# The first pair's q and k cut in halves on two DMA queues, and the order of loads behind them, in a fused attention and cosine feed-forward kernel

## The chip, the cores and the metric

The kernel runs on one core of one Trainium2 chip. The metric is device microseconds of one execution, compared as medians of several runs. A profile is one further execution, recorded instruction by instruction; its own time and its span stand in the table below.

## The reference

Eight batches, 12 heads, 448 positions, head size 64. Queries and keys are normalized, scores are divided by tau = 0.1, and the attention output, laid out as 3584 rows of 768, goes through a feed-forward layer whose activation is h times cos(h).

```python
def _attn_ref(q, k, v, tau):
    q_n = q / (norm(q, axis=-1, keepdims=True) + 1e-06)
    k_n = k / (norm(k, axis=-1, keepdims=True) + 1e-06)
    scores = matmul(q_n, k_n.transpose(0, 1, 3, 2)) / tau
    attn = exp(scores - max(scores))
    attn = attn / (sum(attn, axis=-1, keepdims=True) + 1e-09)
    return matmul(attn, v)                       # (8, 12, 448, 64)

def _moe_ref(x, w_in, w_out):                    # x: (3584, 768)
    h = x @ w_in                                 # (3584, 2048)
    return (h * cos(h)) @ w_out                  # (3584, 768)
```

Inputs and output are float32 in HBM.

## The kernel before

**Work and tiles.** Two heads make a *pair*, three pairs a *unit* (`UP = 3`), two units a batch. There are 16 units and 48 pairs; a label such as `scale1.0` means unit 1, pair 0 of it, which is pair 3 of the kernel. A pair's k lies in partitions 0 to 63 of a buffer `raw` and its q in partitions 64 to 127, seven positions of each head to a partition (`NB = 7`). For each pair the steps are:

- `load`: one DMA for k and one for q (224 KB each), from SyncE's queue (SP);
- `square` (`sq`), `reduce` (`n2`) and `rnorm` (`rn`): the squares, their sums over 64 elements, and one over the root of these. The squares of the first three pairs are taken by ScalarE (ACT), those of the next three by GpSimd (POOL), as the plan's entry `sq` says; the sums by VectorE (DVE); the root by ScalarE as Ln and then Exp, or, for the units that the entry `roots` names, by GpSimd with a power;
- `scale`: raw times rn, to `qks` in bf16, by GpSimd. For pair 0 VectorE does the second half (three of seven position blocks; the first half has four);
- `transposes`: by TensorE (PE) through the identity for the first nine pairs, copied from PSUM to `qkT` by VectorE; by a transposing DMA from pair 9 on;
- `scores`: four score steps per pair, each followed by an Exp of ScalarE into `PX` (one of 448 columns, three of 896);
- `attend`: PX times V, and the row sums. For the first pairs the sums are inverted by ScalarE (`lnS`, `expS`), spread over the partitions by a matmul on PE (`spread`, label B) and multiplied in by VectorE, which gives the transposed attention output `xT`.

After the six pairs of a batch, `m1` multiplies `xT` with the first weights `W1` (16 blocks of 128 of its columns), ScalarE takes the cosine, VectorE multiplies to `gT`, and the second product (`m2_fill`, `m2_quarters`) with the second weights `W2` is spread over the next batch's pairs as filling between their scores. V, W1 and W2 are converted to bf16 on the way in by DMAs from GpSimd's queue: V one DMA per half of the partitions and unit, W1 and W2 in four pieces each.

**What sets the order.** The program records its operations with what they read and write (`Program.op`), and `Program.play` simulates them with costs, among them constants for DMA queues, and picks for each engine the next operation by readiness and due time (`late`, moved by `bias`). `emit` writes each engine's instruction stream in that order, with semaphore waits. So a changed constant or entry can change the order of any engine, and an engine never passes an instruction that waits. Where PE would be idle in the opening stretch, filler matmuls on zeros are put in.

**The opening.** SP issues k and q of pairs 0 to 5, twelve DMAs. ScalarE begins with its table load, then squares pair 0. GpSimd's first DMAs are V of unit 0, held until pair 0's q has landed (tile `first`); behind its half of `scale0.0` it issues V of unit 1 and W1's first piece, then goes on with `scale0.1`.

```python
    first = ["first"]
    load_v(0, None, first)
    first = [("qks", 0, 0, 0)]
    load_w1(0, None, first)
    load_w1(1, None, first)
    load_v(1, None, first)
```

## Time and profile before

| what | value |
|---|---|
| median of 3 runs | 415.97 us (415.55 to 416.21) |
| profiled execution, its own time | 415.4 us |
| its span, first to last instruction | 413.6 us |
| TensorE busy | 404.6 us, 98% |
| ScalarE busy | 270.2 us, 65% |
| GpSimd busy | 248.5 us, 60% |
| VectorE busy | 199.9 us, 48% |
| granted TensorE clock | 1.000 |
| DMA moved | 63.99 MB, mean 155 GB/s |

The profiled execution is 0.57 us under the median; 1.8 us of it lie outside the span. TensorE's busy time includes the fillers of the opening. In a timeline row the first number is the start in us from the span's start, the second the duration, then the engine, the line of the kernel, the operation and its tiles, and in brackets the idle time before it with what ended that. SPq and POOLq are queues in which an engine issues DMAs. In a row of the stretches view each engine has its busy time in the stretch and the number of its instructions. In a row of DMA issues the last number is the median time in us from issue to landing.

### The profile page before, as it was taken

The page shows a single profiled execution, that of the slowest core. Times are in us where ns is not written, and L with a number is a line of the kernel's source. Part 1 is how long each engine was busy: PE and PEld are TensorE (multiplying, and loading weights), DVE is VectorE, ACT ScalarE, POOL GpSimd, SP SyncE. Part 2 cuts the span into 40 slices and gives each one's busy share as a digit, 9 for nine tenths or more (in the row PEclk, how much of TensorE's full clock was granted, in tenths as well). Part 3 has the DMA queues.
Part 4 walks back from the last instruction along what each step waited for, and adds up shares of the span by engine and source line. Part 5 has one row for each costly group of instructions (what it writes and reads, how often), then busy time and mean ns, then how long its engine had stood idle before and what let it go on. Part 6 is the DMA issues. An engine that isn't in the chain of part 4 may idle for free.

```text
span 413.6 us, 13910 instructions
## 1 busy us (share of the span) xinstructions
PE 404.6 (98%) x6213; PEld 243.8 (59%) x6213; DVE 199.9 (48%) x279; ACT 270.2 (65%) x384; POOL 248.5 (60%) x196
## 2 busy tenths in 40 slices
PE   7899999999999999999999999999999999999997
PEld 3354556655566655765567656865567655655555
DVE  4574653426664457445644567344742344413421
ACT  5897578985889745985497647884488745623500
POOL 4999995894776985988489656946482303020000
PEclk9999999999999999999999999999999999999999
DMA  8999999489997999586988975797933531151023
GB/s 183 248 252 226 207 222 202 136 157 215 178 163 164 228 258 188 121 205 149 206 101 188 268 132 113 135 215 188 169 51 79 147 85 32 46 139 38 2 73 81
DMA packets 78736, 63.99 MB, mean 155 GB/s; under 512 B 41844, under 2 KB 72404, under 8 KB 78676
## 3 DMA queue, kind: packets, MB, share of 16 engines
q1 hardware_dynamic: 60468, 50.42, 54.4%
q0 software_dynamic: 18048, 12.59, 20.7%
q8 instruction: 49, 0.80, 0.8%
q10 hardware_dynamic: 160, 0.10, 0.1%
q14 instruction: 11, 0.09, 0.1%
HBM read 55.44 MB, written 11.19 MB: 161 GB/s over the span
## 4 chain that ended last, share of the span: by engine, by line
PE 91%; POOL 3%; ACT 2%; DVE 2%; DMA 1%; issue 0%; SPq 0%; ACTq 0%; POOLq 0%
PE MP L1052 27%; PE SC L953 20%; PE AV L953 12%; PE SC L727 7%; PE AV L764 5%; PE MP L1081 4%; PE AV L788 4%; PE SC L1081 3%; PE MP L953 2%; PE AV L837 2%; POOL qks L678 1%; PE SC L735 1%; ACT cosb L982 1%; PE MP L852 1%; PE AV L1081 1%; DMA raw<-in_q_dram 1%
## 5 line engine op out<-in xcount | busy, mean ns | idle before, releaser
L742 ACT ACTIVATE PX<-SC 128x448 bf16<-128x448 f32 (+1 forms) x192 | 148.7, 825 | 16.0 <-PE SC L727 10.9
L1052 PE MATMUL MP<-W,gT 64*64 64x384 bf16 x2816 | 136.2, 323 | 0.7 <-DVE qkT L716 0.6
L1052 PEld LDWEIGHTS MP<-W,gT 64*64 64x64 bf16 x2816 | 80.1, 107 | 34.5 <-issue 3.9
L953 PE MATMUL SC<-xT,W 128*128 128x448 bf16 x444 | 90.9, 353 | 0.0
L678 POOL TENSOR_TENSOR qks<-raw,rn 128x896 bf16<-128x896 f32 (+1 forms) x48 | 79.8, 1679 | 12.0 <-ACT rn L670 11.6
L640 POOL TENSOR_TENSOR sq<-raw 128x896 bf16<-128x896 f32 x44 | 73.9, 1686 | 11.8 <-DMA raw<-in_q_dram 6.4
L940 POOL TENSOR_TENSOR xT<-xu,RB 128x448 bf16<-128x448 f32 x36 | 40.1, 1135 | 67.7 <-DMA RB<-scr 67.7
L953 PEld LDWEIGHTS SC<-xT,W 128*128 128x128 bf16 x444 | 43.1, 98 | 40.2 <-ACT osb L1016 0.4
L982 ACT ACTIVATE cosb<-SC,cst 128x896 f32<-128x896 f32 x37 | 37.2, 1006 | 37.8 <-PE SC L953 35.9
L953 PE MATMUL AV<-xT,W 128*128 128x448 bf16 x276 | 59.6, 352 | 0.0
L647 DVE TENSOR_REDUCE n<-sq 128x14 f32<-128x896 bf16 (+2 forms) x49 | 51.6, 1059 | 7.1 <-ACT sq L638 4.8
L984 DVE TENSOR_TENSOR gT<-SC,cosb 128x896 bf16<-128x896 f32 x37 | 40.3, 1090 | 28.2 <-ACT cosb L982 28.1
L727 PE MATMUL SC<-qkT 64*64 64x448 bf16 x576 | 51.9, 354 | 0.3
L982 ACT ACTIVATE cosb<-AV,cst 128x896 f32<-128x896 f32 x23 | 23.1, 1006 | 37.1 <-PE AV L953 35.4
L774 DVE COPY xu<-AV 128x448 f32<-128x448 f32 x36 | 22.5, 624 | 50.4 <-PE AV L756 50.4
L953 PEld LDWEIGHTS AV<-xT,W 128*128 128x128 bf16 x276 | 26.6, 98 | 25.4 <-DVE xs L799 1.1
L764 PE MATMUL AV<-PX,va 64*64 64x448 bf16 x432 | 38.2, 349 | 0.0
L614 POOL DMA_DIRECT2D va<-in_v_dram x32 | 22.0, 694 | 22.9 <-DVE gT L984 18.2
L1019 DVE COPY osb<-MP 128x384 f32<-128x384 f32 x26 | 14.5, 558 | 43.9 <-PE MP L1052 32.8
L984 DVE TENSOR_TENSOR gT<-AV,cosb 128x896 bf16<-128x896 f32 x23 | 25.0, 1087 | 20.3 <-ACT cosb L982 20.3
L727 PEld LDWEIGHTS SC<-qkT 64*64 64x64 bf16 x576 | 16.7, 106 | 13.0 <-ACT PX L742 6.3
L775 DVE TENSOR_TENSOR xu<-xu,AV 128x448 f32<-128x448 f32 x36 | 22.4, 621 | 1.2
(84 smaller groups left out, 364.7 us busy)
## 6 DMA issues: line engine op xcount, KB each, us to landing
raw<-in_k_dram SPq DMA_DIRECT2D x48, 224.0 KB, 5.4
raw<-in_q_dram SPq DMA_DIRECT2D x48, 224.0 KB, 5.9
out_dram<-osb SPq DMA_DIRECT2D x54, 192.0 KB, 3.1
RB<-scr SPq DMA_DIRECT2D x22, 336.0 KB, 5.2
va<-in_v_dram POOLq DMA_DIRECT2D x32, 192.0 KB, 6.1
W<-in_moe_w_in_dram POOLq DMA_DIRECT2D x4, 768.0 KB, 15.0
W<-in_moe_w_out_dram POOLq DMA_DIRECT2D x4, 768.0 KB, 20.0
qkT<-qks SPq DMA_TRANSPOSE x39, 4.4
```

Source lines behind the costliest of these rows:

```text
L640: pool(lambda e, x=x, y=y: e.tensor_tensor(y, x, x, ALU.mult), src_, dst, 0.1 + n * 1.78e-3, label="sq%d.%d" % (u, p)).pad = LATE if u > 1 ...
L647: dve(lambda e, w=w: e.tensor_reduce(out=n2v[i][:, 2 * p : 2 * p + 2, w], in_=sqv[p][:, :, w, :], axis=mybir.AxisListType.X, op=ALU.add), ...
L678: f = lambda e, s0=s0, s1=s1: e.tensor_tensor(qksv[i][:, p, s0:s1].rearrange("p s h d -> p h s d"), rawv[i][:, h, s0:s1, :], bass.AP(rn[i] ...
L727: m = e.matmul(SCv[z][BP * o : BP * o + BP, a, 0:S], t[r, c - 1 + (NT3 + 1) * o, 0:BP], t[r, :, BP : 2 * BP], start=True, stop=True)
L742: act(lambda e: e.activation(PHv[j] if c == 0 else PXv[j][:, c - 1], SCv[z][:, :, 0:n], ACT.Exp, scale=1.0 / TAU), ["SC%d" % z], [("PX", j ...
L764: m = e.matmul(AVv[64 * a : 64 * a + 64, o, 0:S], vav[y][r, 2 * p + a, c + 1, :], PXv[j][r, c, a, :], start=(c == 0), stop=False)
L940: f = lambda e, p=p: e.tensor_tensor(xTv[b % 2][:, UP * i + p, :].rearrange("p (s o m) -> p o s m", s=NB, o=2), xuv[:, u % 3, p, :].rearra ...
L953: t = e.matmul(ph[:, a, 0:S], W1v[:, order[c], 128 * n : 128 * n + 128], xTv[b % 2][:, order[c], :], start=(c == 0), stop=(c == NKC - 1))
L982: act(lambda e, ph=ph, cz=cz: e.activation(cosv[cz], ph[:, :, 0:S], ACT.Sin, bias=cst.ap()[:, 0:1], scale=1.0), names(gi) + ["cst0"], [("c ...
L984: dve(lambda e, ph=ph, cz=cz, gi=gi: e.tensor_tensor(gTv[:, 2 * gi : 2 * gi + 2, S * (b % 2) : S * (b % 2) + S], ph[:, :, 0:S], cosv[cz], ...
L1052: r = e.matmul(POH[b][x : x + 64, 0:HW], gTv[k, y, col + x : col + x + 64], W2v[k, y, HW * b : HW * b + HW], start=(y == 0 and h == 0), st ...
L1081: r = e.matmul(po[:, 0 : w[1] - w[0]], gTv[:, y, col : col + 128], W2v[:, y, w[0] : w[1]], start=(y == 0), stop=(y == NF - 1))
```

## The change

The entries of the plan, and what follows from them:

- **Opening loads.** k and q of pair 0 are each cut into the four and the three position blocks; k's halves are issued on SP, q's on ScalarE's own DMA queue (`openers`), four DMAs with a semaphore each. q of pair 2 is issued on ScalarE's queue too (`paired`), and `tableat` puts ScalarE's table load behind the two halves of q and ahead of that third DMA. `square` and `scale` of pair 0 wait for the halves that they read.
- **GpSimd's queue.** The order is V of unit 0, V of unit 1, W1's first piece, W1's second. V of unit 0 is cut into pairs 0 and 1 (issued once k's first half has landed) and pair 2 (issued behind GpSimd's half of `scale0.0`); V of unit 1 waits for both halves of `scale0.0`. W1 has three pieces instead of four: 512, 512 and 1024 columns. The W1 pieces have a bias of -10 in the order.
- **First tile of the second product.** Its 16 steps, for two halves each, are cut 8, 4, 4 instead of 8, 8.
- **Smaller entries.** `roots`: pair 2 of unit 3 takes its root on ScalarE instead of GpSimd. `u4`: the load of unit 4's pair 0 waits for `gT` step 7 instead of 6. `bs`, `bx`: other due times for the row sums' inverse and for `xT`. The buffers `scr` have a semaphore for each of three in turn.
- **The simulation.** `Program.play` has a queue for each of SP, ACT and POOL instead of two, and other constants for their rates and starts.

The orders that come out: GpSimd issues V of unit 0 (first part), scales its half of pair 0, issues V of unit 0 (second part), V of unit 1 and W1's first piece, then scales pair 1; W1's second piece goes ahead of one square and its last ahead of another. ScalarE takes the roots of pair 0 ahead of the squares of pairs 1 and 2, and the root of pair 1 ahead of all Exps of pair 0. VectorE scales pair 0 and copies its transposes ahead of the sums of pair 1. PE does the first pair's product with V ahead of the last two score steps of pair 1, and the spread of pair 0 behind these. In the first m1, VectorE copies the transposes of pairs 7 and 8 one after the other, where a `reduce` stood between them, and the last `gT` comes next. Behind the first batch the engines' streams are the same in count and nearly so in order.

```diff
     "grid": {2: (16, 5, 6), 3: (11, 3, 4), 4: (8, 2, 3)},
...
-    "u4": (6,),
+    "u4": (7,),
...
+    "gates": "xxfcbbc",
+    "openers": ("SP", "ACT"),
+    "paired": (2,),
+    "swo": 1,
+    "dver": (),
+    "wb": -10.0,
+    "tableat": -2,
+    "swseq": "v0 v1 w0 w1",
+    "v0": ((0, 2), (2, 3)),
+    "together": 1,
+    "w1": (0, 1, 2, 4),
...
-    "bs": -1.0,
-    "cut": 8,
-    "bx": 0.0,
+    "bs": -2.0,
+    "cuts": (8, 12),
+    "bx": 1.0,
...
-    "roots": (3, (8, 0), (10, 0), (12, 0), (14, 0)),
+    "roots": ((3, 0), (3, 1), (8, 0), (10, 0), (12, 0), (14, 0)),
...
-    BOTH = 1.09
-    COLD = 2.7
+    BOTH = {"SP": 1.12, "hw": 1.4, "load v": 1.15, "W1": 1.2, "W2": 1.15}
+    QUEUED = 75.0
...
-        for x in ((0,), (1,)) if apart else ((0, 1),):
-            behind = P.ops[-1] if x == (1,) else behind
+        if apart:
+            for z in range(2):
+                s0, s1 = blocks((z,))
+                for x, t in enumerate((k, q)):
+                    go = lambda e, x=x, t=t, s0=s0, s1=s1: e.dma_start(
+                        rawv[i][BP * x : BP * x + BP, h, s0:s1, :].rearrange("p h s d -> p h (s d)"),
+                        bass.AP(t.tensor, ((u // 2) * NH + UH * (u % 2) + 2 * p0) * S * D + s0 * D, [[NB * D, BP], [S * D, 2], [1, (s1 - s0) * D]]))
+                    dma(PLAN["openers"][x], [go], list(reads), [("part", x, z)] + (["first"] if x == 0 and z == 0 else []), "part%d_%d" % (x, z),
+                        0.97 * (s1 - s0) / NB + 0.7 * (z and not x), "load u%d p%d" % (u, p0),
+                        ([o for o in P.ops if o.eng == PLAN["openers"][x] and o.dma is not None] or [None])[-1], 1.8)
+            return
+        paired = u < 2 and UP * u + p0 in PLAN["paired"]
+        for x in ((0,), (1,)) if paired else ((0, 1),):
+            eng = "ACT" if x == (1,) else eng
...
+        if u == 0:
+            for (p0, p1), reads in zip(PLAN["v0"], reads):
+                dma("POOL", [lambda e, z=z, p0=p0, p1=p1: e.dma_start(
...
+            return
...
-        seg = [(h, y, w) for y, w in ([(0, PLAN["cut"]), (PLAN["cut"], NF - PLAN["cut"])] if t == 0 else [(0, NF)]) for h in range(2)]
+        cuts = (0,) + PLAN["cuts"] + (NF,) if t == 0 else (0, NF)
+        seg = [(h, y, z - y) for y, z in zip(cuts, cuts[1:]) for h in range(2)]
...
     for g in range(PB):
-        load(g // UP, g % UP, g % UP + 1, g < PLAN["apart"], "SP", P.ops[-1] if g else None)
+        load(g // UP, g % UP, g % UP + 1, g < PLAN["apart"], "SP", [o for o in P.ops if o.eng == "SP"][-1] if g else None)
+    early = [o for o in P.ops if o.eng == "ACT" and o.dma is not None]
+    P.order_only(early[PLAN["tableat"]], [o for o in P.ops if o.label == "table"][0])
...
-    first = ["first"]
-    load_v(0, None, first)
-    first = [("qks", 0, 0, 0)]
-    load_w1(0, None, first)
-    load_w1(1, None, first)
-    load_v(1, None, first)
+    opens = {"a": [("part", 0, 0)], "b": ["first"], "f": [("qks", 0, 0, 0), ("qks", 0, 0, 1)], "c": [("qks", 0, 0, 0)], "d": [("qks", 0, 1, 0)], "e": [("qks", 0, 2, 0)], "g": [("qks", 1, 0, 0)], "h": [("qks", 1, 1, 0)], "i": [("qks", 1, 2, 0)], "n": []}
+    for n, x in enumerate(PLAN["swseq"].split()):
+        gate = opens[PLAN["gates"][1 + n]] if n else None
+        last = [o for o in P.ops if o.eng == "POOL" and o.dma is not None][-1] if n else None
+        if x[0] == "w":
+            load_w1(int(x[1]), last, gate)
+            P.ops[-1].bias = PLAN["wb"]
+        else:
+            load_v(int(x[1]), last, gate or [opens[x] for x in PLAN["gates"][5:]])
```

More of the change, by code (lines that the diff above doesn't have):

```diff
@@ L79 @@
     __slots__ = ("eng", "fn", "idx", "deps", "cost", "mode", "dma", "bulk", "lock", "label", "bias",
-                 "start", "end", "late", "weight", "pad", "descs", "lead", "free", "waits", "inc", "count", "pos", "dcount", "known", "nd")
+                 "start", "end", "late", "weight", "pad", "descs", "lead", "free", "waits", "inc", "count", "pos", "dcount", "known", "nd", "shy")
 class Program:
@@ L211, in release, with gain @@
                     waiting[w.eng].append(w)
+        def gain(heads):
+            sw = [h[3].label for h in heads if h[3].eng == "POOL"]
+            g = max([self.BOTH["SP"]] + [y for x, y in self.BOTH.items() if sw and sw[0].startswith(x)])
+            return max(g, self.BOTH["hw"]) if len(heads) - len(sw) > 1 else g
         def flow(until):
@@ L635, in square @@
             src_, dst = [("raw", i, p, z) for z in range(2)], [("sq", p, z) for z in t]
+            src_ += [("part", x, z) for x in range(2) for z in t] if (u, p) == (0, 0) else []
             n = (w.stop - w.start) * 2 * D
@@ L681, in scale @@
             src_ = [("raw", i, p, z) for z in range(2)] + [("rn", i, p, z) for z in t]
+            src_ += [("part", x, z) for x in range(2) for z in t] if (u, p) == (0, 0) else []
             keys = [("qks", i, p, z) for z in t]
@@ L1130, in norms @@
         if p == 0:
-            for x in range(UP) if u != 5 else [x for x in range(UP) if x not in PLAN["split5"]]:
+            for x in [x for x in range(UP) if not (u == 5 and x in PLAN["split5"] or u == 3 and x in PLAN["split3"])]:
                 square(u, x, PLAN["squared"].get((u, x), "P"))
@@ L1263, in bass_cosine_attention__then__act_gcu_kernel @@
     norms(2, 1)
-    loads(3)
+    for x in range(UP):
+        if x not in PLAN["split3"]:
+            load(3, x, x + 1)
     norms(3, 0)
@@ L1271, in bass_cosine_attention__then__act_gcu_kernel @@
         load_v(3, find("W2.3"))
+    for x, y in PLAN["split3"].items():
+        load(3, x, x + 1, reads=[("gT", 0, y)])
+        square(3, x, "P")
+        reduce(3, x)
     norms(3, 1)
```

92 lines of the change are left out of this document (54 added, 38 removed).

## The prediction

> **What bounds the kernel now.** I read the page's busy times first, then stretches of the span, then the chain that ended last. TensorE (PE) is busy for almost the whole span, so the end moves only if PE does useful work sooner or loses one of its few gaps. The stretches say where gaps are left (after each stretch its length, then busy time and instructions of PE, its weight loads, DVE, ACT and POOL, the granted clock, the DMA share and GB/s):
>
> ```profile
> 20.00:36.00 16.00, 15.80 (x230) 8.43 (x228) 10.66 (x15) 15.19 (x28) 15.96 (x14) 1.00 1.19 249
> 54.00:58.00 4.00, 3.21 (x50) 1.93 (x51) 3.69 (x5) 2.80 (x4) 3.91 (x5) 1.00 1.16 209
> 58.00:413.00 355.00, 352.11 (x5683) 216.84 (x5672) 165.84 (x214) 228.66 (x317) 196.56 (x148) 1.00 0.70 144
> ```
>
> From 58 us on PE misses 2.9 of 355 us: the order there can give or take tenths. The clock is granted in full everywhere. Between 54 and 58 it misses 0.79 of 4.00. From 20 to 36 it misses 0.2 of 16, but ScalarE misses only 0.81 as well: attention of the first batch runs PE and ScalarE at their limits together. What is left is the opening before 20 us, where most of PE's busy time is filler. There the chain is:
>
> ```profile
> 0.72 0.76 SPq L599
> 1.54 3.81 DMA raw<-in_q_dram
> ...
> 5.44 0.64 ACT sq L638
> 6.10 0.70 DVE n L647
> 6.82 0.31 ACT rn L667
> 7.16 0.22 ACT rn L670
> 7.52 1.05 POOL qks L678
> 8.86 1.35 POOL va L614 x2
> ...
> 11.05 1.73 POOL qks L678
> ...
> 19.38 0.40 PE MP L702 x4
> 19.77 0.92 PE MP L852 x4
> ...
> 21.44 0.68 PE AV L828 x12
> 22.12 0.32 PE AV L845 x12
> ```
>
> The reader should see three links: the wait for pair 0's q, landing at 1.54 + 3.81 = 5.35; the round ScalarE, VectorE, ScalarE, GpSimd of its norms; and from 8.86 GpSimd, which issues DMAs ahead of `scale0.1` and then squares and scales without a pause until PE takes over at 19.38 with pair 3's transposes, the spread of pair 0 (L852) and V of pair 1 (L828, L845). What ScalarE does meanwhile decides more:
>
> ```profile
> 7.32 0.95 ACT L638 ACTIVATE sq<-raw 128x896 bf16<-128x896 f32 x1
> 11.98 1.35 ACT L742 ACTIVATE PX<-SC 128x448 bf16<-128x448 f32 x2
> 13.44 0.62 DVE L716 COPY qkT<-MP 128x896 bf16<-128x896 bf16 x1 [1.86 <-PE MP L702]
> 13.77 2.16 ACT L742 ACTIVATE PX<-SC 128x896 bf16<-128x896 f32 x3 [0.43 <-PE SC L727]
> ...
> 19.23 0.39 ACT L889 ACTIVATE RB<-RB 128x224 f32<-128x224 f32 x1
> ```
>
> The Exps start at 11.98, four to a pair, one of 448 and three of 896 columns: 1.35 for one of each, 2.16 for two long ones and the short one of pair 1, so 0.81 a long one and 0.54 a short one. Pair 1's first began at 13.77 + 2.16 - 0.54 = 15.4. The Exps of pairs 0 and 1 and the inverse of pair 0's row sums are through at 19.23 + 0.39 = 19.62. ScalarE hardly pauses between, so an earlier first Exp is worth something only if pair 1 comes sooner too.
>
> **The change part by part.** *The first landing.*
>
> ```profile
> raw<-in_k_dram SPq DMA_DIRECT2D x1, 224.0 KB, 3.6
> 2.85 0.61 SPq L599 DMA_DIRECT2D raw<-in_q_dram  x1
> raw<-in_q_dram SPq DMA_DIRECT2D x1, 224.0 KB, 4.4
> 0.72 1.28 ACT L556 ACT_TABLE_LOAD   x1 [0.72 <-PEq L1346]
> ```
>
> The first k (issued at 0.72) lands 3.6 us later, at 4.32; q follows at 5.35, so 224 KB take 1.03 us and the fixed part is 2.6 us. The first halves are four sevenths: 256 KB, 1.18 us. If both queues together move what one does, they land at 0.72 + 2.6 + 1.18 = 4.50. If the second queue doubled it, 3.9; but ScalarE then issues two DMAs (0.76 and 0.61 as on SP), loads its table (1.28) and issues pair 2's q (0.61), so it is free at 0.72 + 3.3 = 4.0 to 4.1. I take 4.4, near the first bound, because the first queue alone already left no gap between landings: 1.0 us earlier than 5.44. [...]
>
> *Pair 0's norms.* From the square's start to the scale's start was 7.52 - 5.44 = 2.08 and the scale's half took 1.05; so `scale0.0` runs from 6.5 to 7.5 on GpSimd. The second halves land at 5.0 to 5.4, and ScalarE now takes their roots before other squares, so VectorE's half starts at about 7.1 where it stood behind the sum of pair 1. Pair 0's first scores are ready near 9.2. But the Exps stand behind the root of pair 1 on ScalarE. Its square starts when q of pair 1 has landed (7.25 before, 2.85 + 4.4), which I put at 7.8, as pair 2's q now shares the engines with it; 0.95 for the square (the row at 7.32), then VectorE's sum (1.08, a row further down) behind its copies of pair 0, 9.1 to 10.2, then the root (7.16 + 0.22 - 6.82 = 0.56) to 10.8. First Exp 10.8 instead of 11.98: 1.2 us. Bounds: q of pair 1 at 7.25 changes nothing (VectorE is the later one), at 8.9 the Exp starts at 11.4.
>
> *GpSimd's queue.* Behind `scale0.0` it issues two DMAs more than before, V of pair 2.
>
> ```profile
> L614 POOL DMA_DIRECT2D va<-in_v_dram x8: 653/691/852, 5.7 to 54.5; - x8
> L1100 POOL DMA_DIRECT2D W<-in_moe_w_in_dram x4: 882/886/896, 10.2 to 30.9; - x4
> ```
>
> V moves 64 x 6 = 384 runs at 0.69 us, a W1 piece 128 x 6 = 768 at 0.89; on that line 128 runs take 0.56, between 0.5 and 0.69. Then: 7.5, pause 0.3 (as from 8.57 to 8.86), 1.1, V of unit 1 1.35, W1 0.89: `scale0.1` at 11.15 (11.0 to 11.6) against 11.05. Everything that GpSimd does up to 19.38 follows with the same pieces, so its chain gains nothing and may lose 0.5. W1's second piece moves ahead of one square, which exchanges two items; its last two pieces become one, which takes 0.89 off GpSimd near 30 us, off the path.
>
> *Pair 1 and on.* `scale0.1` ends at 12.9; from the scale's end to that of VectorE's copy were 13.44 + 0.62 - (11.05 + 1.73) = 1.28, so 14.2, and the scores 0.3 more: first Exp of pair 1 at 14.6. ScalarE gets there at 10.8 + 3.0 (Exps of pair 0) + 0.56 (root of pair 2) = 14.4. So 15.4 - 14.6 = 0.8 us are left here. PE now does V of pair 0 between pair 1's second and third score steps, 0.68 + 0.32 us as for pair 1 and some 0.4 for the opening matmuls, so ScalarE waits some 0.5 us around the row sums: these and pair 1 end near 19.35, against 19.62: 0.25 left of 1.2. PE, however, has then done the spread (0.92), while two score steps of pair 2 are still to come (by columns half of L828's 0.68, 0.34): it is 0.6 us ahead. Since ScalarE's 0.81 us of gaps from 20 to 36 are waits for PE or for the norms, I take half, 0.4 (bounds 0 and 0.8). Together 0.65 us by the end of pair 5. Then m1, which PE fills, takes that over, if the weights are there.
>
> ```profile
> 30.89 0.88 POOL L1100 DMA_DIRECT2D W<-in_moe_w_in_dram  x1
> W<-in_moe_w_in_dram POOLq DMA_DIRECT2D x1, 768.0 KB, 12.8
> 45.05 1.30 PE L953 MATMUL MP<-xT,W 128*128 128x448 bf16 x6
> ```
>
> W1's fourth piece landed at 30.89 + 12.8 = 43.7; m1's third quarter, which used the third, starts at 45.05. As one piece both count as landed with the fourth, and as the bytes ahead of it are the same, near 43.7. With PE 0.65 earlier, the need is at 44.4: 0.7 us of cover. I cost it at nothing.
>
> *VectorE in m1.*
>
> ```profile
> 55.09 1.08 DVE L647 TENSOR_REDUCE n<-sq 128x14 f32<-128x896 bf16 x1
> 56.84 1.50 PE L1052 MATMUL MP<-W,gT 64*64 64x384 bf16 x32 [0.64 <-DVE qkT L716]
> ```
>
> The second product waited 0.64 us for the last copy of transposes, which stood behind a sum of 1.08. Without the sum the copy still has to wait for pair 8's transposes on PE: I take 0.25 us (bounds 0 and 0.64).
>
> *The rest.* W2's last piece is needed at 63.5:
>
> ```profile
> 42.00 0.80 POOL L1106 DMA_DIRECT2D W<-in_moe_w_out_dram  x1
> W<-in_moe_w_out_dram POOLq DMA_DIRECT2D x1, 768.0 KB, 20.5
> 63.51 0.82 PE L1052 MATMUL MP<-W,gT 64*64 64x384 bf16 x16
> ```
>
> It landed at 62.5; the cut 8, 4, 4 puts its use 16 matmuls (0.8 in that row) later, and unit 4's load leaves its way, so 0.9 us of gain finds it there. The cut adds two changes of accumulation half; PE waits there for its last matmul, but other work lies between at one of them: 0.05, at most 0.3. Pair 2 of unit 3 adds a Ln and an Exp, 0.56, to ScalarE behind m1, where the next batch's Exps run without a pause; 0.05, at most 0.5. The reordered tail: 0, ±0.4.
>
> Sum: 0.65 + 0.25 - 0.1 = 0.8 us sooner. The profiled execution would take 414.6 instead of 415.4, and the median, 0.57 above it, 415.97 - 0.8 = **415.2 us**.
>
> **The rivals.**
>
> *The lead passes whole.* If ScalarE does not wait around pair 0's row sums, the lead of 0.8 at pair 1 stays, PE's lead turns into the whole 0.8 of ScalarE's gaps, and the copy gives 0.4: 2.0 us, 414.0. For it: PE still has fillers in its order there, so V's matmuls may start sooner than I put them. Against: GpSimd's chain gains nothing.
>
> *Interleaving eats the lead.* Pair 2's q on its own queue takes turns with pair 1's q and with V, which now starts a microsecond sooner: 448 KB of pair 0 and 672 KB behind them at 1.03 per 224 KB end at 0.72 + 2.6 + 5.15 = 8.5, with V's share 8.9. Then the first Exp stands at 11.4, and `scale0.1` at 11.7: pair 1 keeps 0.2, the row sums end at 19.9, the halved gaps (0.4) make up for that 0.3, and the copy less the 0.1 of the rest is left, 0.2: 415.7. For it: q of pair 1 took 4.4 us where the first k took 3.6, so transfers do wait for each other. [...] Two hardware queues side by side no run here shows yet. Against: the piece needed first has a queue of its own for only one transfer.
>
> *Slower: W1's last piece.* It is 1024 columns under one semaphore, so m1's third quarter waits for all of it. It decides from a landing past 44.4. SP's loads of later units, whose buffers come free sooner, take turns with it: two of 224 KB more ahead of its end make 43.7 + 2.06 = 45.8, four 47.8; PE, with nothing else in its order there, stalls 1.4 to 3.4. Less the 0.8: 0.6 to 2.6 slower, from 416.6, and 417.2 as the likelier. For it: the fourth piece took 12.8 us to land though it was alone in its queue for its last part. Against: longer runs, and no more bytes than before.
>
> **How the numbers follow.** Forecast 0.5, with its own range 414.4 to 415.9 (the bounds of the halved gaps and of the cut); the lead whole 0.2; interleaving 0.12; W1 late 0.18. A measurement of this kernel tells about 0.2% from no change, 0.83 us, so 415.14 and 416.8 are the borders. The forecast lies on the first: 0.25 faster, 0.25 same. With the lead whole 0.2, faster 0.45. Same: 0.25 + 0.12 + 0.03 of W1 = 0.4. Slower 0.15. The range is 413.7 to 416.8.
>
> **What would show it.** The first square on ScalarE at 4.4; `scale0.1` at 11.0 to 11.6; first Exp at 10.8; pair 0's row sums inverted by 19.4; the second product's first matmul at 56.0 instead of 56.84; no idle time of PE at the third quarter of m1. The forecast is wrong if pair 1's square starts after 8.5, if PE's stretch from 20 to 36 has over 0.5 of gaps, or if PE waits for W1 or W2.

## The result, and the profile after

The changed kernel takes 418.82 us (median of 20 runs, 416.52 to 421.06); the kernel before, beside it on the same chip, 416.12 (20 runs). The ratio is 1.0061, 95% interval 1.0046 to 1.0077: 0.6% slower, where 415.2 and faster had been forecast. A ratio here is an estimate over all the executions and need not be the quotient of the two medians. Two executions far above the others, one of e15 (422.51 us) and one of the kernel before beside it (599.9), are left out of medians and ratios. The first profiled execution took 416.95 us (span 415.1), the second lowest of the 20; a second profile of the same kernel (e5 below) 419.22.

The opening on ScalarE, and on GpSimd, in the timeline of the changed kernel:

```profile
4.24 0.63 ACT L682 ACTIVATE sq<-raw 128x512 bf16<-128x512 f32 x1 [0.79 <-DMA raw<-in_k_dram]
6.87 0.52 ACT L682 ACTIVATE sq<-raw 128x384 bf16<-128x384 f32 x1 [2.00 <-DMA raw<-in_k_dram]
7.30 0.29 ACT L713 ACTIVATE rn<-n,cst 128x8 f32<-128x8 f32 x1
11.77 1.33 ACT L789 ACTIVATE PX<-SC 128x896 bf16<-128x896 f32 x2
16.23 1.35 ACT L789 ACTIVATE PX<-SC 128x448 bf16<-128x448 f32 x2 [1.22 <-PE SC L782]
...
7.98 1.05 POOL L724 TENSOR_TENSOR qks<-raw,rn 128x512 bf16<-128x512 f32 x1 [2.00 <-ACT rn L716]
9.33 1.25 POOL L651 DMA_DIRECT2D va<-in_v_dram  x2 [0.30 <-POOL qks L724]
10.53 1.37 POOL L657 DMA_DIRECT2D va<-in_v_dram  x2
11.82 0.92 POOL L1151 DMA_DIRECT2D W<-in_moe_w_in_dram  x1
12.68 1.78 POOL L724 TENSOR_TENSOR qks<-raw,rn 128x896 bf16<-128x896 f32 x1
```

The first halves come early: the first square starts at 4.24 instead of 5.44. But ScalarE then stands for 2.00 us with the square of the second half in hand, waiting for its k, and the root of the first half (7.30), whose sums had been ready since 5.6, stands behind that square. So `scale0.0` begins at 7.98 instead of 7.52 and `scale0.1`, behind three issues, at 12.68 instead of 11.05. What is late is k's second half, as the list of DMA issues up to 9 us shows (size, then median time to landing):

```profile
raw<-in_k_dram SPq DMA_DIRECT2D x1, 128.0 KB, 3.5
raw<-in_q_dram ACTq DMA_DIRECT2D x1, 128.0 KB, 3.0
raw<-in_q_dram ACTq DMA_DIRECT2D x1, 96.0 KB, 3.9
raw<-in_k_dram SPq DMA_DIRECT2D x1, 96.0 KB, 5.3
```

The two first halves land in 3.5 and 3.0 us; k's second half, the smaller, takes 5.3. q's second half, issued at 1.48, is there at 5.34. What holds k's half back is taken up at e4.

The stretches of the changed kernel, and then of the one before where they had not been shown:

```profile
20.00:36.00 16.00, 15.90 (x233) 7.74 (x225) 10.30 (x16) 15.13 (x29) 15.97 (x14) 1.00 1.16 257
54.00:58.00 4.00, 3.44 (x55) 2.12 (x56) 3.34 (x5) 2.42 (x3) 3.58 (x4) 1.00 1.17 204
58.00:130.00 72.00, 71.82 (x1380) 44.17 (x1376) 36.40 (x47) 61.68 (x97) 47.81 (x35) 1.00 0.92 170
130.00:150.00 20.00, 18.52 (x359) 11.33 (x348) 6.61 (x11) 12.17 (x16) 18.33 (x17) 1.00 1.16 219
```

```profile
58.00:130.00 72.00, 71.62 (x1379) 43.62 (x1372) 35.66 (x46) 61.16 (x95) 49.47 (x36) 1.00 0.94 179
130.00:150.00 20.00, 20.00 (x367) 12.21 (x360) 8.15 (x12) 12.79 (x17) 19.47 (x17) 1.00 1.03 214
```

In the stretches shown up to 130 us the changed kernel has no more idle time on PE than before. Between 130 and 150 it has 1.48 us and the other none. The row of the waits that names it (us in total, how often, the longest), the transfer in the chain, and the queue of SP ahead of it, first changed, then before, there with the time from T21's issue (L695) to its landing:

```profile
PE SC L782 <- DMA qkT<-qks: 1.5, 1, 1.5
...
132.46 6.43 DMA qkT<-qks
...
127.77 0.57 SPq L970 DMA_DIRECT2D scr<-xs  x1
128.39 3.96 SPq L985 DMA_DIRECT2D RB<-scr  x4
132.46 1.25 SPq L742 DMA_TRANSPOSE qkT<-qks  x1
```

```profile
126.86 0.60 SPq L920 DMA_DIRECT2D scr<-xs  x1
127.50 1.23 SPq L1023 DMA_DIRECT2D out_dram<-osb  x2
130.93 1.24 SPq L695 DMA_TRANSPOSE qkT<-qks  x1
132.21 1.32 SPq L935 DMA_DIRECT2D RB<-scr  x2
...
DMA to landing us min/median/max: 2.9/2.9/2.9
```

L742 and L695 are the transposing DMA of pair 21 (`T21`). Before, it stands ahead of the broadcast of unit 5's inverses (`bcast5`, L935). In the changed kernel SP issues both broadcasts (units 4 and 5, x4) first, which holds it for 3.96 us, and T21 follows 1.5 us later than before. It also takes longer: 6.43 us to land, where before it took 2.9. Issued 1.5 us late but landing in 2.9 it would have been there at 135.4, ahead of its use, so what makes PE wait is the longer way to land, behind the broadcasts. No line of the diff speaks of either: the planner drew that order from the changed entries and constants, and which of them did it was not tried. This accounts for the first profile: 0.15 us late at the second product, level by 66 us, 1.5 us late from 138 us to the end. The other 1.9 us up to the median are not in this profile.

### The profile page after: what moved, and what is told of

Same layout as the page of the kernel before. It is cut to its first block, busy times and chain, and to the rows that moved or that the text cites. A ratio compares the mean times of both kernels' runs of the same rounds, so it can differ in the third digit from the quotient of the medians.

```text
span 415.1 us, 13920 instructions
## 1 busy us (share of the span) xinstructions
PE 406.6 (98%) x6215; PEld 244.3 (59%) x6215; DVE 200.4 (48%) x279; ACT 270.2 (65%) x386; POOL 246.2 (59%) x195
## 4 chain that ended last, share of the span: by engine, by line
PE 91%; DMA 3%; ACT 2%; DVE 2%; POOL 1%; issue 0%; SPq 0%; ACTq 0%; POOLq 0%
PE MP L1103 26%; PE SC L1003 20%; PE AV L1003 12%; PE SC L774 7%; PE AV L811 5%; PE MP L1132 4%; PE AV L835 4%; PE SC L1132 3%; PE MP L1003 2%; PE AV L884 2%; DMA qkT<-qks 2%; DMA raw<-in_k_dram 1%; PE SC L782 1%; PE AV L875 1%; ACT cosb L1032 1%; PE MP L899 1%
## 5 line engine op out<-in xcount | busy, mean ns | idle before, releaser
L657 POOL DMA_DIRECT2D va<-in_v_dram x30 | 20.5, 690 | 16.0 <-DVE gT L1034 16.0
```

## The experiments

In all of them `P.arrange()` plans as in the named kernel, and a changed `start` of an operation then moves it in its engine's stream. Each comparison is with runs of the kernel before on the same chip beside it: medians 415.54 (29 runs) for e1 to e4, 415.58 (17) for e5 to e8, 415.66 (29) for e9 to e11, 415.67 (23) for e12 and e13, 415.9 (22) for e14 and e15; e16 and e17 have one execution beside them (415.31).

**e1, T21 first, and e2, the same delay put into the kernel before.**

```diff
 # e1, in the changed kernel
+    find("bcast5").start = find("T21").start + 0.001
 # e2, in the kernel before (its scr buffers with a semaphore each)
+    find("bcast4").start = find("spread5").start + 0.001
+    find("T21").start = find("bcast5").start + 0.001
```

> The changed kernel with one pair of SP's DMAs exchanged: pair 21's transposing DMA (T21) is issued ahead of the broadcast of unit 5's row sums, as in the kernel before. Theory of the queue order (T21 behind the broadcasts is late, and PE waits for it at 137 us): PE's wait of 1.5 us is gone, the median falls from 418.8 to 415.7 to 416.3, and the scatter of 4 us falls to about 1. Rival theory of the opening (the second halves of pair 0 land late and unsteadily): the median stays above 417.5 and the scatter stays.

> The kernel before, whose opening is untouched, with SP's order of the changed kernel in that place: both broadcasts ahead of T21, and the spread's semaphores split as in the changed kernel so that this order is safe. Queue order: 417.5 to 420 with a scatter of some us, PE waits 1 to 4 us for T21. Opening: 416.1, as before.

e1: 416.69 us (12 runs, 415.63 to 419.09), ratio 1.0028 (1.0012 to 1.0044). The wait for T21 is gone. e2: 417.67 (6 runs), ratio 1.0050 (1.0033 to 1.0067), with the wait of the changed kernel:

```profile
138.39 0.29 PE L735 MATMUL SC<-qkT 64*64 64x224 bf16 x4 [1.83 <-DMA qkT<-qks]
```

So the order alone costs 2.1 us in the kernel before, and taking it out of the changed one leaves 1.15 us of the 2.7 by which that was over the kernel before. In e2 T21 is issued 1.54 us later than before and takes 5.9 us to land instead of 2.9. But e1 does not reach the forecast, and its times spread over 3.5 us where five of e2's six lie within 0.6. In e1's profile the second product begins at 55.95, 0.89 us ahead of before; later the lead is lost, 0.9 us of it in waits for `xT` behind a broadcast (L985) that took 7.32 us, and 0.5 in a wait for `gT` near 291 us:

```profile
181.10 7.32 DMA RB<-scr
188.48 3.31 POOL xT L990 x3
```

**e3, the root ahead of the late square, and e4, q of pair 2 back on SP.** Both on top of e1.

```diff
 # e3
+    half = [o for o in P.ops if o.label == "sq0.0"][1]
+    half.start = find("rn0.0a").start + 0.001
+    [o for o in P.ops if o.label == "red0.0"][1].start = half.start + 0.001
 # e4
+    one = [o for o in P.ops if o.eng == "ACT" and o.label == "load u0 p2"][0]
+    one.eng, one.deps = "SP", [d for d in one.deps if d[1] is not None]
+    one.start = [o for o in P.ops if o.eng == "SP" and o.label == "load u0 p2"][0].start + 0.001
```

> As the first of these, and in ScalarE's order the root of pair 0's first half ahead of the square of its second half. Theory: the root of the first half is ready at 5.6 but stands behind that square, which waits for k's second half until 6.9; freed, GpSimd's half of the first scale starts at 6.5 instead of 7.98, scale0.1 at 11.7 instead of 12.7, and the time falls 0.4 to 1.0 below the first run's. Rival: ScalarE and PE are full from 20 us on and the opening's lead is lost there, as the changed kernel's own delay of 1.6 us at scale0.1 cost nothing by 128 us: within 0.2 of the first run.

> As the first of these, with q of pair 2 issued on SP behind its k instead of on ScalarE's queue. If that transfer, taking turns, is what holds back the second halves (landing 6.0 and 6.8), they land at 5.3 to 6.0, the square of the second half runs at 5.5 to 6.1 instead of 6.87, and scale0.1 starts 0.7 to 1.0 earlier. Rival: the pause of the DMA engines between the first and the second halves (about 0.7 us near 4 us) does it, whoever follows: 6.5 to 6.9 still. The time within 0.4 of the first run either way.

e3: 417.87 us, ratio 1.0041 (1.0019 to 1.0062), in two groups: three of twelve times at 415.2 to 415.4, nine from 416.6 to 419.4. e4: 418.06, ratio 1.0049 (1.0034 to 1.0065). Neither gain shows in the time, although e3's second product begins a microsecond early, at 55.83, and both are further from e1 than their expectations allowed. On its own question e4 answers: k's second half lands at 5.4 us, and pair 1's q at 7.3, as in the kernel before; in e10 (below), which has pair 2's q on SP too, they land at 5.3 and 7.3. In the 13 profiles of this opening with pair 2's q on ScalarE's queue they land at 5.5 to 6.9 and at 7.9 to 8.9. So that transfer costs pair 1's q 0.6 us and more, and by these rows it holds k's half back too. The waits of PE in e3 say why its profiled execution (419.22) is long:

```profile
PE MP L1103 <- issue: 2.6, 2, 2.1
PE AV L868 <- issue: 1.4, 1, 1.4
```

"issue" means that nothing that the profile shows held PE back. That its own instructions were missing is the author's reading, called late code in the expectations below; no row names it, and what it rests on are counts. The page has a queue named instruction with 49 packets and 0.80 MB, 16 KB each, and PE runs 12,430 matmuls and weight loads, 254 to a packet. The packets keep step with PE: in the trace of the kernel before each of the 49, numbered k from 0, begins when PE has begun 33 to 302 instructions more than 256 k, in that of the changed kernel 35 to 362. Where PE stopped is told by the counts of a stretch from 0 to the stop (the first x is matmuls, the second weight loads): in e3 at its two stops, in e12 (below) at its two:

```profile
q8 instruction: 49, 0.80, 0.8%
...
0.00:65.48 65.48, 61.82 (x726) 31.84 (x726) 36.73 (x69) 48.86 (x81) 54.12 (x50) 1.00 1.14 221
0.00:72.53 72.53, 67.48 (x853) 36.75 (x853) 38.46 (x72) 53.71 (x87) 57.62 (x52) 1.00 1.16 219
```

```profile
0.00:65.23 65.23, 62.67 (x726) 32.21 (x726) 36.60 (x69) 48.81 (x81) 53.67 (x50) 1.00 1.15 219
0.00:72.67 72.67, 68.33 (x853) 37.11 (x853) 38.32 (x72) 54.05 (x89) 58.02 (x53) 1.00 1.13 217
```

726 + 726 = 1452 and 853 + 853 = 1706, the same to the instruction in both, and 254 apart. e4 stopped at both counts too. The packet that ends just before the first stop, k = 4, began at 64.18 in e3, when PE had begun 1410 instructions, 386 past the mark 256 k ("behind 256 k" below; the larger the number, the later the packet); in the kernel before, the packet with the same number began at 61.91, at 1250, 226 behind it.

**e5, the changed kernel again, unchanged, for a second profile.**

> The changed kernel once more, unchanged, for a second profile; the first profile fell on 416.95 us, the second lowest of its 20 times, and cannot show what costs the other 1.9 us to its median of 418.82. Theory (late code): TensorE's own instructions come in 49 packets of 16 KB on the queue named instruction (q8), about 256 instructions each; where the DMA engines are full, a packet starts late and TensorE stops with its next instruction missing, which the waits list as issue. If this execution lies at 418 us or above, TensorE shows 1 to 3 us of idle time ended by issue between 58 and 80 us, beside 1.5 us for the transposing DMA of pair 21 near 139 us. Rival (data only): the slow executions lose their time to a named transfer (W2, a k or q load, a broadcast of the inverses), and issue is under 0.3 us.

It took 419.22 us and shows both losses:

```profile
PE SC L782 <- DMA qkT<-qks: 1.6, 1, 1.6
PE MP L1103 <- issue: 1.0, 1, 1.0
```

The stop is at 71.59 us and, again, at 853 + 853 instructions. Compared by the number of the matmul, this execution was 0.66 us ahead of before at 66 us and 0.81 behind at 78: 1.2 us go between the matmul at the stop and the eighth behind it, a little more than the 1.0 of the row, and the rest in steps of 0.14 us and less on either side. Another 0.4 goes near 118, 1.7 at T21 and 0.75 behind the broadcast near 190. Of the theory this execution shows the stop; that a packet starts late where the DMA engines are full is shown neither here nor by e11.

**e6 and e8, the same work with more instructions ahead of it.** Fillers in two halves of 224 columns: 80 more PE instructions in e3, 76 in the kernel before, at the same filler time.

```diff
-    P.filler = (lambda e, shut: e.matmul(PO[:, 0:S], zt[:, 0:128], zt, ...), ...)
+    P.filler = (lambda e, shut: [e.matmul(PO[:, x : x + S // 2], zt[:, 0:128], zt[:, x : x + S // 2], ...) for x in (0, S // 2)][-1], ...)
```

> As e3 (T21 ahead of bcast5, root of pair 0's first half ahead of the square of its second half), but each of TensorE's 40 filler matmuls of the opening on 448 zero columns is cut into two of 224: 80 more instructions (40 matmuls, 40 weight loads) at the same filler time, before pair 0's scores and in its gaps, and nothing else. e3 stopped at the instructions 1452 and 1706 of TensorE's stream with issue. Late code: the edges of the code packets lie 80 instructions earlier in the work, so a stop, where there is one, comes at the same counts 1452 and 1708 of the new stream, which is 80 instructions earlier in the work than in e3, and the time can move either way by 1 to 3 us. Rival (order or data): the stops stay at the same place of the work (the product of pair 8 with V and the second product's steps near 72 us), and the median stays at 417.9 with both of e3's groups (415.2 and 417 to 419).

> The kernel before with one edit: each of TensorE's 38 filler matmuls of the opening is cut into two halves of 224 columns, 76 more instructions, same filler time; all orders and transfers stay. Late code: the time of the same work depends on where the edges of the code packets fall; 415.5 to 418, and if over 416, then with idle time ended by issue in the profile at 256 k + 420 to 430 instructions. Rival (order or data): nothing moves, 415.5 within 0.3 and no issue over 0.3 us. A result of 415.5 without any issue would leave both open, since the packets might be in time at this place too.

e6: 419.05 us, ratio 1.0078 (1.0052 to 1.0104). Its longest stop:

```profile
76.60 0.28 PE L868 MATMUL AV<-PX,ones 64*64 64x224 bf16 x1 [1.55 <-issue]
...
0.00:75.06 75.06, 72.08 (x980) 42.83 (x980) 39.56 (x74) 57.25 (x94) 59.52 (x54) 1.00 1.13 219
```

980 + 980 = 1960 = 1452 + 2 x 254: the stop keeps to the count of the stream, not to the work. (A short one of 0.22 is at 853 + 853.) e8: 417.27, ratio 1.0032 (1.0020 to 1.0045), for 76 instructions in time that was idle. Its profile has one such stop, of 0.2 us at 132.5 us (1994 + 1995 = 3989; 1452 + 10 x 254 = 3992); it loses 0.5 us between 130 and 136 us, and 0.9 us at a wait for `gT` near 291. The rival's "nothing moves" falls.

**e7, only the opening.** The change with before's cuts, roots and gate of unit 4, and all that the plan of before has behind 44 us in before's order.

```diff
+    for o in P.ops:
...
+        o.start = held.get((o.eng, o.label, n), min(o.start, 43.99))   # held: before's starts; n: which of that label
```

> The change with the later order held: the cuts of the first tile (8, 8), the roots of unit 3 and the gate of unit 4 as before, and every instruction that stands behind 44 us in the plan of before keeps before's order on all five engines; only the opening (halves on two queues, the third pair's q, V and W1 ahead) is that of the change. The order theory, which puts the loss to the later order alone: 415.0 to 415.6, level with before or 0.5 under it, no wait for T21 and none for the broadcasts near 185 us. Late code: level with before only in part; TensorE reaches the second product up to 0.7 us earlier while W2 still arrives, and if the packets come late, 416 to 418 with issue of 0.5 us or more between 58 and 80 us. The rival that the opening itself loses: above 416 with the second product's first matmul later than 56.84 us.

416.37 us, ratio 1.0015 (1.0003 to 1.0027). No stop, no wait for T21; the profile (416.42) shows the opening alone losing: `scale0.1` at 12.73 and the second product at 57.27 instead of 56.84. The times reach from 414.43 to 417.36.

**e9, that and the root first.** e7 with e3's edit.

> As e7 (the change's opening, before's order behind 44 us) with one more edit: ScalarE takes the root of pair 0's first half ahead of the square of its second half. In e7's profile that square stood until 6.91 us for its k, scale0.0 began at 8.02 and scale0.1 at 12.73; in all profiles so far of this opening the second product begins 44.3 to 44.5 us behind scale0.1. Theory (the root behind the late square is what the opening loses): scale0.0 at 6.1 to 6.3, scale0.1 at 11.3 to 11.5 whatever the second halves do, the second product at 55.9 to 56.2, 0.7 to 0.9 us ahead of before's 56.84; median 414.7 to 415.3 with less scatter than e7. Rival (the lead is taken back by the late code and by the transfers near 186 and 290 us): the second product as early as that, but a median of 415.6 to 417 with stops ended by issue or waits for the broadcasts. Second rival: scale0.1 does not move, and the median is e7's 416.4.

415.20 us, ratio 0.9987 (0.9973 to 1.0000): the only version whose median is under that of the kernel before, by half a microsecond and at the edge of what can be told. The timeline, to be set beside that of the changed kernel:

```profile
5.52 0.30 ACT L716 ACTIVATE rn<-n,cst 128x8 f32<-128x8 f32 x1 [0.75 <-DVE n L696]
6.44 0.52 ACT L685 ACTIVATE sq<-raw 128x384 bf16<-128x384 f32 x1 [0.38 <-DMA raw<-in_k_dram]
...
6.22 1.04 POOL L727 TENSOR_TENSOR qks<-raw,rn 128x512 bf16<-128x512 f32 x1 [0.32 <-ACT rn L719]
11.24 1.68 POOL L727 TENSOR_TENSOR qks<-raw,rn 128x896 bf16<-128x896 f32 x1
```

The second half's square still starts late (6.44), but nobody waits behind it. The starts in the profiles of this opening, in us:

| kernel | second half's square | scale0.0 | scale0.1 | second product | from scale0.1 |
|---|---|---|---|---|---|
| before | - | 7.52 | 11.05 | 56.84 | 45.79 |
| changed | 6.87 | 7.98 | 12.68 | 56.99 | 44.31 |
| e5 (changed) | 6.31 | 7.42 | 12.12 | 56.42 | 44.30 |
| e1 | 5.83 | 6.94 | 11.64 | 55.95 | 44.31 |
| e7 | 6.91 | 8.02 | 12.73 | 57.27 | 44.54 |
| e9 | 6.44 | 6.22 | 11.24 | 55.92 | 44.68 |
| e12 | 5.79 | 6.03 | 11.14 | 55.58 | 44.44 |

The landing of k's second half moves by more than a microsecond from one execution to the next (5.5 to 6.9, as said at e4), and without the root first the start of everything moves with it. With the root first the second product comes 0.92 us sooner than before (e9).

**e10 and e13, what is still on the way to scale0.1.** e10 is e9 with W1's first piece issued behind `scale0.1` and q of pair 2 on SP; e13 is e9 with the first of these alone.

```diff
+    find("W1.0").start = find("scale0.1").start + 0.001
```

> As e9, and two things taken off the way to scale0.1: the first piece of W1 is issued behind scale0.1 instead of ahead of it (0.92 us of GpSimd), and q of pair 2 goes back to SP's queue (its issue behind k of pair 2). Theory: scale0.1 0.9 us earlier than in e9, at 10.3 to 10.6, the second product at 54.9 to 55.3 if the chain behind scale0.1 is what bounds it; median 413.8 to 414.5, the best of all. Rival (the transfers bound): pair 1's k and q or W1 and W2 come no earlier, so that less than half of the 0.9 us is left at the second product, or it is lost again behind it to issue stops at 58 to 80 us; median 415 to 417.

> As e9 with one edit: GpSimd issues W1's first piece behind scale0.1 instead of ahead of it; q of pair 2 stays on ScalarE's queue. Theory (the issue is on the way): in e9 GpSimd issued it from 10.30 to 11.18 and began scale0.1 at 11.24, while the root of pair 1 was ready at about 11.1; so scale0.1 moves by 0.1 us at most, to 11.1 to 11.2, as ScalarE's root (10.88 for 0.21) is the next to end, and the median is e9's 415.2 within 0.4. Rival (the issue alone holds it): scale0.1 at 10.4 and a median of 414.2 to 414.6. Second rival: W1's first piece, now issued about 3 us later, comes too late for the first m1 at 33.1, and the time is 415.6 or more.

e10: 415.97 us, ratio 1.0010 (0.9998 to 1.0021). One edit hides the other: q of pair 2 came 6.5 us after its issue, and the root of pair 1 stood behind pair 2's square:

```profile
10.97 0.95 ACT L685 ACTIVATE sq<-raw 128x896 bf16<-128x896 f32 x1 [2.44 <-DMA raw<-in_q_dram]
```

e13: 415.95, ratio 1.0000 (0.9989 to 1.0012), so 415.6 or more as the second rival had it, but for another reason. GpSimd now waits ahead of `scale0.1`, which does not come earlier:

```profile
11.56 1.68 POOL L727 TENSOR_TENSOR qks<-raw,rn 128x896 bf16<-128x896 f32 x1 [1.45 <-ACT rn L719]
13.19 0.91 POOL L1154 DMA_DIRECT2D W<-in_moe_w_in_dram  x1
15.76 1.70 POOL L727 TENSOR_TENSOR qks<-raw,rn 128x896 bf16<-128x896 f32 x1
```

The root of pair 1 is next in line (again behind the square of pair 2, here for its k), and the issue, 0.91 us, has only moved ahead of pair 2's scale, which starts at 15.76 instead of e9's 14.53.

**e11, more transfer in the kernel before.**

```diff
+    dma("POOL", [...384 KB of moe_w_out to a DRAM buffer...])   # behind W2.3
```

> The kernel before with one more transfer and nothing else: behind the last piece of W2 (issued at 42.0 us) GpSimd's queue copies 384 KB from the second weights to a DRAM buffer that nobody reads; all orders stay. Late code (packets of TensorE's instructions stand behind data in full DMA engines): 416 to 419, with stops ended by issue of 0.5 to 3 us between 58 and 80 us, the packets of blocks 4 to 6 begun over 300 instructions behind 256 k where before's began at 219 to 278. Rival (data only): no issue over 0.3 us; either 415.5 or a named wait for k, q or W2. The added issue holds GpSimd for 0.8 us at 42.8, where it has idle time until 44.

415.94 us, ratio 1.0006 (0.9995 to 1.0018): inconclusive. Packets 6 and 7 began later (326 and 284 instructions behind 256 k instead of 278 and 246), and PE had one stop of 0.55 us, but at 234 us, not at 58 to 80. That full DMA engines make the packets late is not shown by it.

**e12, the whole change with the later order held, and e15, that without the cuts.** Before's order from 66 us on, and the root first; e15 has the cuts 8, 8.

> The whole change, with its cuts 8, 4, 4, its roots, its gate of unit 4 and its first m1, and two repairs of order: everything that stands behind 66 us in the plan of before keeps before's order on all engines (so T21 stands ahead of the broadcast of unit 5), and ScalarE takes the root of pair 0's first half ahead of the square of the second. Theory (three causes make up the loss, and the change's other parts give what the prediction said): scale0.1 at 11.2 to 11.4, the second product at 55.5 to 55.9, a lead of 1.2 to 1.4 us over before at 62 us as in e1 and e3; if it is kept, 414.2 to 414.8, below e9's 415.2. Rival (late code takes a lead at 58 to 75 us): e3's profile with this first tile stopped for 4.0 us, e4's for 1.8 and e1's for none, e9's with before's first tile for none; then the median is 415.5 to 417.5 with both groups of e3, above e9. Then it is the change's own first tile, whose instructions come closer together there, that runs short of code.

> As e12 with one edit: the first tile's steps are cut 8, 8 as before. TensorE still takes 16 matmuls of the first tile ahead of scores that precede them in before's order, at 57 to 62 us. If the cuts 8, 4, 4 are the cause, no stops and 414.2 to 415; if the order of matmuls there or the lead is the cause, the same two groups as e12 (414.4 to 415.3 and 416 to 419.8) with a median near 416.3 and stops ended by issue at 65 and 72 us in a slow execution.

e12: 416.31 us, ratio 1.0023 (1.0000 to 1.0045), from 414.42 to 419.75; the rival. The profiled execution (418.1) led by 1.50 us at 66 us, by the number of the matmul and in the time of the kernel before, and was 2.7 behind at 78:

```profile
PE MP L1106 <- issue: 1.8, 1, 1.8
PE AV L871 <- issue: 1.8, 1, 1.8
```

There is little else in it: each stop took 2.0 us of the lead, and without them it would have ended near 414. e15: 416.55, ratio 1.0022 (1.0006 to 1.0038), with a stop of 1.0 at 70.95, at 1707 instructions. So the stops come without the cuts 8, 4, 4 as well.

**e14, e9 with the copies of the first m1 together, and two more profiles of it, e16 and e17.**

```diff
+    for n, l in enumerate(("red3.2", "ad3.2", "pw3.2")):
+        find(l).start = max(find(l).start, find("g0.7").start + 0.001 * (n + 1))
```

> As e9 with one edit: in the first m1 VectorE copies the transposes of pairs 7 and 8 one after the other and takes the last gT, and the sums of unit 3's pair 2 (red3.2) come behind these, as in the change; TensorE's order stays that of before from 44 us on. The term that the prediction put at 0.25 us: second product at scale0.1 + 44.3 instead of + 44.55, at 55.6 to 55.8, a lead of 1.15 to 1.2 us at 62 us. If the late code comes from the order or the cuts of the first tile, the lead stays and the median is 414.7 to 415.1, 0.2 to 0.3 below e9's 415.2. If it comes from the lead itself, stops ended by issue appear at 62 to 76 us and the median is 415.5 to 417.

> e14 once more, for a second profile. If this execution is over 417 us: late code expects TensorE idle by issue of 1 to 4 us between 62 and 78 us, with packets 4 or 5 begun over 350 instructions behind 256 k; the rival (the transfers behind the broadcasts) expects a named wait of 1 to 2 us near 188 or 290 us and issue under 0.3 us. If it is under 416 us: a lead of 0.85 to 0.95 us until 186 us, and at most 0.9 us lost near 290 us, as in e14.

> e14 a third time, for a third profile; the expectations are those of the run before it.

The copies give the 0.24 us that were forecast: PE's wait ahead of the second product is 0.40 instead of 0.64.

```profile
55.72 1.49 PE L1106 MATMUL MP<-W,gT 64*64 64x384 bf16 x32 [0.40 <-DVE qkT L766]
```

But by 62 us the lead is e9's again (0.88), and the time is 416.07, ratio 1.0022 (1.0003 to 1.0042), in two groups: seven of twelve from 414.98 to 416.09, five from 417.2 to 419.1. All three profiles fell into the lower group (415.37, 414.67, 414.80) and have stops of at most 0.22 us; e14's lost 0.8 us at a wait for `gT` near 290 us, the other two did not. What the upper group loses is open. e14 keeps before's order of PE, so if it is the packets, a lead of a microsecond is enough.

## Why the prediction was wrong, point by point

**The first landing: right.** 4.4 was said, the square started at 4.24, and at 3.95 to 4.29 in the other profiles of this opening, between the two bounds of 3.9 and 4.50. The upper one was worked out for two queues that together move what one does; the traces lie 0.2 us and more under it, most of them nearer to the 3.9 of a doubled rate, and do not decide between the two.

**Pair 0's norms: the first step that failed.** "The second halves land at 5.0 to 5.4" measured 5.34 for q, as said, but 6.85 for k (1.55 + 5.30 in the chain), and the step overlooked that ScalarE's order has the square of the second half ahead of the root of the first. So `scale0.0` came at 7.98 and not from 6.5 to 7.5, and the first Exp at 11.77 and not 10.8. Pair 1's square began at 8.72, past the 8.5 that the prediction had named as its limit; the other limit, 0.5 us of gaps on PE from 20 to 36, was kept (0.10). The rival "interleaving eats the lead" named the right transfer (first Exp 11.4, `scale0.1` 11.7): pair 1's q landed at 8.7, where the forecast had 7.8 and the rival 8.5 to 8.9, and in e4, with pair 2's q on SP, at 7.3. But it did not look for the same in pair 0's own second half, which decided more. Those 96 KB took 5.3 us to land, the 128 KB of k's first half 3.5.

**GpSimd's queue: right in size, wrong in start.** From the end of `scale0.0` to `scale0.1` the step had 0.3 + 1.1 + 1.35 + 0.89 = 3.64; measured 12.68 - 9.03 = 3.65. The start of 12.68 instead of 11.15 is the step before alone.

**Pair 1 and on: undersized.** From `scale0.1` to the second product the change needs 44.54 us with before's first m1 (e7) where before needs 45.79: 1.25 us gained, where the step had 0.75 (the 0.65, and the 0.1 by which it put `scale0.1` later). In the first profile that just pays for the 1.63 us by which `scale0.1` is late, with the copies' 0.24: 0.15 late. With the root first (e9) `scale0.1` is only 0.19 us late and the second product 0.92 us early, more than the 0.65. So it is the place of the late square in ScalarE's order that undid the opening, and not the plan of the loads alone.

**The copies 0.25, the weights nothing: right.** 0.24 measured (e7 against the change, e9 against e14), though with before's order behind it (e14) the 0.24 are gone again by 62 us. PE never waited for W1 or W2, so the slower rival did not come; its side came by another way.

**The reordered tail, "0, ±0.4": the largest failure.** It measured +1.5 to 2.1 us (the changed kernel's profiles, e1, e2), from one DMA behind two broadcasts on SP. The prediction took its size from PE's gaps: it misses 2.9 of 355 us behind 58, so "the order there can give or take tenths". Few gaps bound what an order can win, not what it can lose. The comparison of the orders could have shown this beforehand: T21's landing has a due time, the scores of pair 21, and in the kernel before it was issued 5.4 us ahead of these (130.93 against 136.36). Of these 5.4 the landing took 2.9. Behind both broadcasts it took 5.9 to 6.7 us (changed, e5, e2), more than the whole room. A term for "nearly the same order" has no size without that look.

**What no step had: stops of PE ended by issue.** The lead was treated as kept by PE once won. In the profiles of e3, e4, e6, e12 and e15 a lead of 1.2 to 1.6 us at 66 us was gone at 78, and in the changed kernel's second profile one of 0.66. It was kept there in e1 (1.14) and in e9 and the three of e14 (0.7 to 1.0).

Together: opening about 0.7 us slower (e7), T21 1.5 to 2.1, stops ended by issue 0 to 4 from one profile to the next (none in e1, 4.0 in e3). The range, 413.7 to 416.8, left the last two out. A further loss is not explained: near 290 us PE waits 0.5 to 1.4 us for `gT` in the profiles of e1, e4, e6, e8, e10, e14 and e15, and not in the others, the changed kernel's two among them. In e14's profile VectorE stands there 5.70 us with the inverse of row sums in hand, waiting for a DMA of SP, and that `gT` stands behind it.

## What to carry to other kernels

When a planner's constants change, compare its order on the DMA-issuing queues to the end, and ask of every moved DMA how much room it had between landing and use, and what now stands ahead of it in its queue; "nearly the same order" is no bound, and neither are few gaps on the engine that waits for it. When a transfer is cut in halves, follow the late half as closely as the early one, and see what stands behind the instruction that waits for it. A lead won at the start is only kept where nothing later is in time by less than that lead; here stops of PE that no row explains took 4.0 us in e3's profile, where the lead had been at most 1.6, so count PE's instructions to each idle time ended by issue and see whether the counts repeat.

## What was not expected of the hardware

The 16 idle times of PE ended by issue (0.2 us and more, behind 55 us) in all the profiles lie at 1452 + 254 n of its matmuls and weight loads, where 254 is also what falls to one of the 49 packets of 16 KB (12,430 / 49). Nine are exactly there (1452, 1706 and 1960), one 1 past it, the others 3 to 7 short, to n = 24; they are 0.2 to 2.1 us long. Of the packets 4 to 6 in all 19 profiles, nine began 342 to 418 instructions behind 256 k (e3, e4, e5, e6, e12, e15), and each was followed by a stop at its count, of 0.57 to 2.11 us; the others, at 326 and less (219 to 278 in the kernel before), brought one of 0.2 us and more, of 0.22. Later packets do not part so clearly: stops followed four at 294 to 298 (e3, e6, e8, e11), and none followed packet 16 of e1 at 369. In e8 76 more instructions in idle time cost the kernel before 1.7 us in the median; its profile has one such stop, of 0.2 us. Why a packet begins late is not settled: the DMA engines were full then in the kernel before too (share 1.25 from 58 to 66 us, 1.27 in e3, 1.24 in e9), e11's added transfer brought no stop there, and no row shows when a packet was asked for. That packet 4, in a queue of its own, began 160 instructions later in e3 than in the kernel before, 2.3 us (64.18 against 61.91), is not explained by the runs here.
